# Two key chunks per attention visit for pairs 5, 6 and 7, where there was one

## The chip, the cores and the metric

The kernel runs on one core of one Trainium2 chip. The metric is the device time of one execution in microseconds (us); the time before is the median of three runs. The core's engines are TensorE (PE, matmuls; its weight loads are shown as PEld), VectorE (DVE), ScalarE (ACT), GpSimd (POOL) and SyncE (SP, which issues most DMAs). PE writes its results to PSUM, a small memory in banks, from which DVE or ACT must take them before a bank can be used again.

## What is computed

The program is an attention block with a hash mask, followed by a Fourier mixing block with a feed-forward network. All arrays are float32, the weights come in as float64.

```python
batch, n_heads, seq, head_dim = (4, 8, 768, 64)

# attention: a key counts only if its 6 hash bits equal the query's
q_bits = (np.einsum('bhsd,dk->bhsk', q, proj) > 0)
k_bits = (np.einsum('bhsd,dk->bhsk', k, proj) > 0)
mask = q_bucket[:, :, :, None] == k_bucket[:, :, None, :]
scores = np.where(mask, scale * np.matmul(q, k.transpose(0, 1, 3, 2)), -1e9)
attn = softmax(scores)
x = np.matmul(attn, v)            # then (B,H,S,D) -> (B, S, H*D)

# mixing: real part of a 2-D FFT, normalisation, feed-forward 512 -> 2048 -> 512
mixed = np.real(np.fft.fft(np.fft.fft(x, axis=1), axis=2))
u = x + mixed
un = (u - mean(u)) / np.sqrt(var(u) + 1e-06)
out = u + np.maximum(un @ w_ch1, 0.0) @ w_ch2
```

## The kernel before

**Pairs and chunks.** The heads are taken two at a time. There are 4 batches of 4 pairs, so pairs are numbered n = 0 to 15, and batch b has the pairs 4b to 4b+3. The 768 keys of a pair are cut into 6 chunks of 128. For one chunk, `scores` multiplies the keys by all 768 queries, for two query halves g and two heads h: four matmuls (line 894) into two PSUM tiles named `sc`. There are only two such tiles, so one chunk fills them. `weights` (line 905) takes the exponential of each tile on ACT and writes it to a buffer `pk`. `weigh` applies the hash mask on DVE (line 919, one instruction per head): it keeps a weight where the query's bucket number `qb` equals the key's `kb`. For the first pairs (`LITE`, n = 0 to 4) the mask is added on PE instead, by the bfloat16 matmuls of line 886, and line 919 is not run. `chunk` adds the weights to a running sum `acc` (line 1007). `values` multiplies the weights by the values of that chunk, four matmuls (line 930) into the two tiles `oo`. There are two buffers `pk` (`NPK = 2`), used in turn: a chunk's exponentials can start only when the chunk two before it has been through `values` and the sum.

**The end of a pair.** After the sixth chunk `scale` takes `oo` out of PSUM on ACT (lines 941 and 944), adds up the row sums on PE (line 949), turns them into reciprocals on DVE and, in a second part, spreads them with eight small copies on ACT (line 965) and multiplies the result (line 970).

**Visits.** `attention(b)` is a generator that yields once for each chunk. It has two forms of visit, chosen by `n < TWO`, with `TWO = 8`.

- Pairs 0 to 7 use the single form. One visit does the scores of one chunk, the exponentials directly with them (line 899), the mask and the sum, and then the values of the chunk before.
- Pairs 8 to 15 use the double form, at even chunks only. It does the scores of chunk c, the values of the earlier of two waiting chunks, the exponentials and the mask of c, the values of the later waiting chunk, and then the scores of chunk c+1, marked `glued`, with its exponentials and mask. Odd chunks only yield.

Waiting chunks stand in the list `pending`; the single form leaves one there, the double form two.

**What runs beside it.** Between the visits of batch b the steps of the mixing block of batch b-1 are issued (`other`, the generator `mix`): the Fourier transforms (lines 1122, 1151, 1165), the first feed-forward product (`inner`, line 1426, with copies on ACT and additions on DVE, lines 1448 to 1477) and the second (`outer7`, line 1306, with lines 1318 to 1367). Both products use a Strassen-like scheme with seven products. At each yield of `attention` as many steps are issued as keep pace, some 2.5 of them. The next pair's queries and keys are prepared in steps of their own (`prepare`: transposes on DVE, line 768; hash bits, line 825; bucket numbers, lines 839 and 849, evacuated at lines 535 and 537). They use the same `sc` tiles as the scores. In batch 1, and only there, the second weight matrix is also converted from float64: POOL issues the loads (line 693), DVE and ACT convert (`narrow`, lines 639 to 656, among them line 647 on ACT, which reads the freshly loaded data in `zraw`), DVE makes the sums of quarters (lines 1272 to 1275), and the first weight matrix is cut up for the later batches (`quarters`, lines 1224 to 1230).

**What sets the order.** For batch 0 the order is that of the program text (`manual_schedule`). From batch 1 on a planner lays the order of every engine in advance, with estimated durations: an instruction that is ready by its reckoning is taken by priority, and priority is the order of the program. `behind()` ties a matmul behind the last one noted in `last[0]` (`issue_after`) and moves its priority forward by `AHEAD = 500`. The later matmuls of one chunk's scores, the values, and all scores of a glued chunk are tied in this way. On the chip each engine then works through its list in that order.

Of the kernel before, what the change touches and what calls it, by code (L numbers as in the profile page):

```python
# [485 lines left out]
def _main(  # L486
# [381 lines left out]
        with tc.issue_after(last[0].ins), tc.high_priority(offset=AHEAD):  # L868
            yield

    TWO = 8

    def scores(n, c, glued=False):

        qt, kt, qb, kb = preps[n]
        pss = []
        ks = slice(c * P, (c + 1) * P)
        heads = [slice(h * D, (h + 1) * D) for h in range(2)]
        for g in range(2):
            qs = slice(g * HALF, (g + 1) * HALF)  # L880
            ps = ps_sc.tile([P, 2, 512], F32, tag="sc", name=f"sc{n}_{g}_{c}")
            if kb is None:

                at = (c + (NT // 2 if g else 0)) % NT * P
                for h, rows in enumerate(heads):
                    nc.tensor.matmul(
                        ps[:, h, 0:HALF], qb[rows, 1, at : at + P],
                        qb[rows, 0, g * HALF : (g + 1) * HALF],
                        start=True, stop=False,
                    )  # L890

            for h, rows in enumerate(heads):
                with behind() if (g + h or glued) and n >= NPAIR else nullcontext():
                    last[0] = nc.tensor.matmul(  # L894
                        ps[:, h, 0:HALF], kt[rows, ks], qt[rows, qs],
                        start=kb is not None, stop=True,
                    )
            if n < TWO:
                weights(pks[npk[0] % NPK], g, ps)
            pss.append(ps)  # L900
        return pss

    def weights(pk, g, ps):

        nc.scalar.activation(  # L905
            pk[:, g, :, 0:HALF], ps[:, :, 0:HALF], AF.Exp, scale=SCALE
        )

    def weigh(n, c, pss):
# [3 lines left out]
        npk[0] += 1  # L913
        for g in range(2) if n >= TWO else ():
            weights(pk, g, pss[g])
# [56 lines left out]
    def attention(b):  # L972
# [11 lines left out]
        for t in range(NPAIR):  # L984
# [8 lines left out]
            def chunk(c, pss):  # L993

                nonlocal first
                pk = weigh(n, c, pss)
                new = pk[:, :, :, 0:HALF]
                sums = [acc]
                if c == 0:
                    first = new  # L1000
                elif c == NT - 1 and b == 0:

                    sums.append(new)
                else:

                    for g in (0, 1) if b == 0 else (slice(0, 2),):
                        nc.vector.tensor_tensor(  # L1007
                            acc[:, g], (first if c == 1 else acc)[:, g], new[:, g],
                            op=ALU.add,
                        )  # L1010
                return n, c, pk, oos, sums

            for c in range(NT):
                if n < TWO:
                    new = chunk(c, scores(n, c))
# [573 lines left out]
def kernel(tc, *args):  # L1589

    cn = {n: tc.nc.inline_tensor(a, name="k_" + n) for n, a in _consts().items()}
    with ExitStack() as ctx:
        large = _main(ctx, tc, *args, cn)
    with tc.If(large > 0, preferred_fallthrough_block=True):
        _any_scores(tc, *args, cn)
# [34 lines left out]
```

## Time and profile before

| | us |
|---|---|
| median of 3 runs | 1098.16 (1097.16 to 1098.83) |
| profiled execution | 1095.54 |
| its span, first to last instruction | 1093.6 |
| PE busy in the span | 1034.4 |
| DVE busy | 788.6 |
| ACT busy | 499.2 |
| score matmuls, line 894 (768 passes) | 153.5 |
| value matmuls, line 930 (768 passes) | 149.2 |
| exponentials, line 905 (192) | 146.8, 0.81 each |
| mask multiplies, line 919 (132) | 129.1, 1.01 each |

A line of the page or of an answer names the line of the program, the engine and the operation, then what is written and what is read, with buffer numbers left out. Each float32 matmul is counted as two passes, so a chunk's four score matmuls are "x8". Matmuls overlap in the pipeline, so what one costs is read from start to start. In a list of waits the columns are the total, the number and the longest wait. In a timeline they are the start, the duration, the instruction, and in brackets the idle time before it with what ended it.

### The profile page before, as it was taken

The numbers are of one execution on the slowest core, as the hardware profiler recorded it, in microseconds if no ns is written. First come the engines' busy times: TensorE is split into PE (matmuls) and PEld (weight loads), VectorE is DVE, ScalarE is ACT, GpSimd is POOL, SyncE is SP. The second block draws the span as 40 slices with busy tenths as digits, with TensorE's granted clock in tenths as the row PEclk, the third lists the DMA queues.
The fourth block names the chain that finished last, engine by engine and source line by source line (L and its number), as shares of the span: only waits on it lengthen the run. The fifth ranks groups of instructions, "written<-read, shape, count | busy, mean of one in ns | idle before, by whom it ended". The sixth has DMA issues, their size and how long they took to land.

```text
span 1093.6 us, 14135 instructions
## 1 busy us (share of the span) xinstructions
PE 1034.4 (95%) x4933; PEld 633.6 (58%) x4933; DVE 788.6 (72%) x1336; ACT 499.2 (46%) x1055; POOL 58.3 (5%) x132
## 2 busy tenths in 40 slices
PE   7989897999989999999999999999999999999996
PEld 3333354446744676545664576645675579768675
DVE  5899968868599978694857786876765875644353
ACT  6987556653276324354325424354415522340420
POOL 0000000002000020010000011001000002100000
PEclk9999999999999999999999999999999999999998
DMA  9755352440056162223063224213123205122401
GB/s 233 216 97 126 63 145 67 164 149 11 20 155 207 43 206 40 54 57 84 15 181 85 63 63 159 44 36 91 25 82 113 76 20 173 54 82 84 129 20 42
DMA packets 175711, 103.14 MB, mean 94 GB/s; under 512 B 129552, under 2 KB 162960, under 8 KB 175632
## 3 DMA queue, kind: packets, MB, share of 16 engines
q1 hardware_dynamic: 169840, 88.65, 30.2%
q0 software_dynamic: 4224, 13.11, 3.8%
q8 instruction: 41, 0.67, 0.2%
q10 hardware_dynamic: 1568, 0.39, 0.2%
q14 instruction: 38, 0.31, 0.1%
HBM read 81.14 MB, written 20.97 MB: 93 GB/s over the span
## 4 chain that ended last, share of the span: by engine, by line
PE 57%; DVE 16%; ACT 4%; issue 2%; DMA 2%; DVEq 0%; ACTq 0%
PE o L1306 23%; PE h_p L1426 18%; PE oo L930 5%; PE sc L894 5%; DVE pk L919 5%; DVE acc L1007 3%; PE cs L1122 2%; DMA zraw<-in_moe_w_ch_dram 2%; PE A L1151 1%; PE B L1151 1%; ACT pk L905 1%; ACT rr L965 1%; PE bits L825 1%; DVE x L1165 1%; DVE h L1464 0%
## 5 line engine op out<-in xcount | busy, mean ns | idle before, releaser
L1306 PE MATMUL o<-w,h 128*128 128x256 f32 x1152 | 258.5, 381 | 2.0 <-DVE w L1318 0.8
L1306 PEld LDWEIGHTS o<-w,h 128*128 128x128 f32 x1152 | 216.8, 190 | 41.8 <-issue 3.5
L905 ACT ACTIVATE pk<-sc 128x768 f32<-128x768 f32 x192 | 146.8, 808 | 93.4 <-PE oo L930 30.6
L1426 PE MATMUL h_p<-x,w 128*128 128x384 f32 x448 | 162.4, 492 | 2.2 <-ACT h L1448 1.7
L894 PE MATMUL sc<-qt,kt 64*128 64x384 f32 x768 | 153.5, 502 | 5.9 <-ACT pk L905 5.6
L930 PE MATMUL oo<-pk,vn 128*64 128x385 f32 (+1 forms) x768 | 149.2, 499 | 6.8 <-DVE pk L919 4.4
L919 DVE SCALAR_TENSOR_TENSOR pk<-qb,kb,pk 128x768 f32<-128x768 bf16 x132 | 129.1, 1010 | 34.3 <-ACT pk L905 34.0
L1426 PEld LDWEIGHTS h_p<-x,w 128*128 128x128 f32 x448 | 82.5, 190 | 67.1 <-issue 6.5
L1007 DVE TENSOR_TENSOR acc<-acc,pk 128x1536 f32<-128x1536 f32 (+1 forms) x72 | 105.7, 1482 | 5.7 <-ACT pk L905 5.1
L1426 PE MATMUL h_p<-w 128*128 128x384 f32 x288 | 106.4, 492 | 3.5 <-ACT w L1463 2.3
L930 PEld LDWEIGHTS oo<-pk,vn 128*64 128x64 f32 x768 | 50.7, 136 | 95.0 <-issue 73.3
L894 PEld LDWEIGHTS sc<-qt,kt 64*128 64x128 f32 x768 | 66.4, 186 | 56.8 <-ACT pk L905 19.1
L1426 PEld LDWEIGHTS h_p<-w 128*128 128x128 f32 x288 | 53.0, 190 | 45.5 <-ACT w L1475 5.1
L1318 DVE SCALAR_TENSOR_TENSOR w<-o,rs,w 128x256 f32<-128x256 f32 x56 | 26.7, 477 | 42.4 <-PE o L1306 42.4
L1336 ACT COPY tq<-o 128x256 f32<-128x256 f32 x24 | 8.9, 372 | 101.8 <-PE o L1306 101.8
L1306 PE MATMUL o<-w 128*128 128x256 f32 x176 | 42.0, 381 | 0.3 <-DVE w L1318 0.3
L1459 DVE TENSOR_TENSOR h<-h 128x384 f32<-128x384 f32 x32 | 17.7, 552 | 29.5 <-ACT h L1458 29.5
L1452 DVE TENSOR_TENSOR h<-h 128x384 f32<-128x384 f32 x32 | 17.7, 553 | 26.8 <-ACT h L1451 26.7
L1306 PEld LDWEIGHTS o<-w 128*128 128x128 f32 x176 | 33.0, 190 | 6.8 <-issue 1.1
L1060 POOL DMA_DIRECT2D out_dram<-w x30 | 16.4, 548 | 376.4 <-ACT tq L1336 146.2
L1325 ACT COPY tq<-o 128x256 f32<-128x256 f32 x24 | 8.9, 369 | 58.4 <-PE o L1306 58.3
L1122 PE MATMUL cs<-ch,z 128*128 128x128 f32 (+3 forms) x192 | 31.7, 317 | 3.0 <-DVE bt L829 1.9
(170 smaller groups left out, 1311.4 us busy)
## 6 DMA issues: line engine op xcount, KB each, us to landing
w<-ad SPq DMA_DIRECT2D x168, 128.0 KB, 2.0
w<-bd SPq DMA_DIRECT2D x42, 512.0 KB, 4.5
zraw<-in_moe_w_ch_dram POOLq DMA_DIRECT2D x16, 512.0 KB, 4.0
bd<-w SPq DMA_DIRECT2D x14, 512.0 KB, 4.2
vn<-in_v_dram SPq DMA_DIRECT2D x32, 192.0 KB, 3.4
qn<-in_q_dram SPq DMA_DIRECT2D x120, 48.0 KB, 2.3
kn<-in_k_dram SPq DMA_DIRECT2D x60, 96.0 KB, 3.1
zraw<-in_moe_w_ch_dram SPq DMA_DIRECT2D x8, 512.0 KB, 5.9
```

The lines of the kernel that those rows point to most:

```text
L894: last[0] = nc.tensor.matmul(ps[:, h, 0:HALF], kt[rows, ks], qt[rows, qs], start=kb is not None, stop=True,)
L905: nc.scalar.activation(pk[:, g, :, 0:HALF], ps[:, :, 0:HALF], AF.Exp, scale=SCALE)
L919: nc.vector.scalar_tensor_tensor(w, qb[:, h].rearrange("p (g s) -> p g s", g=2), kb[:, h, c : c + 1], w, op0=ALU.is_equal, op1=ALU.mult,)
L930: oo = nc.tensor.matmul(oos[g][h * D : (h + 1) * D, 0:w], nat["v", n][:, (2 * c + h) * D : (2 * c + h + 1) * D], pk[:, g, h, 0:w], start=( ...
L1007: nc.vector.tensor_tensor(acc[:, g], (first if c == 1 else acc)[:, g], new[:, g], op=ALU.add,)
L1122: nc.tensor.matmul(ps[:, pc + 2 * lo : pc + 2 * hi - 1 : 2], z[:, cp, pc, par, t * P : (t + 1) * P], ch[:, cp, pc, lo:hi], start=(cp == 0) ...
L1151: nc.tensor.matmul(ps[:, cols], F[:, par, k, t, j * P : (j + 1) * P], sq[:, t, k, cols], start=(t == 0), stop=(t == 1),)
L1306: nc.tensor.matmul(ps, a[:, r], right7[i][:, r], start=start and r == 0, stop=r == HF // 2 - 1, skip_group_check=not start,)
L1318: nc.vector.scalar_tensor_tensor(t[:, cols], src, r, t[:, cols], op0=ALU.mult, op1=ALU.add)
L1426: nc.tensor.matmul(ps, left[:, k], right[i][:, k], start=start and k == 0, stop=k == 1, skip_group_check=not start,)
L1452: nc.vector.tensor_tensor(c21, c12, c21, op=ALU.add)
L1459: nc.vector.tensor_tensor(c22, c21, c22, op=ALU.add)
```

## The change

The bound between the two forms of visit moves from pair 8 to pair 5. Pairs 5, 6 and 7, which are all of batch 1 but its first pair, take the double form. Pair 4, whose mask is added on PE, stays with the single form. The tests `n < TWO` in `scores` (exponentials with the scores) and `n >= TWO` in `weigh` (exponentials there) follow the same constant.

```diff
-    TWO = 8
+    TWO = 5
```

At the passage from pair 4 to pair 5 one chunk is waiting, not two; the double form's first `finish()` (`if len(pending) > 1`) is then left out for that visit. At the end of batch 1 two chunks are waiting, and the loop after the pairs takes them both.

## The prediction

> **What bounds the kernel now.** I read the page's busy table first, then the list of what TensorE (PE) waited for in the stretch that changes, then the same list one batch later, where the new visit form already runs, and last the timelines of one visit of each form.
>
> ```profile
> PE 1034.4 (95%) x4933; PEld 633.6 (58%) x4933; DVE 788.6 (72%) x1336; ACT 499.2 (46%) x1055; POOL 58.3 (5%) x132
> ...
> PE 57%; DVE 16%; ACT 4%; issue 2%; DMA 2%; DVEq 0%; ACTq 0%
> ```
>
> PE is busy for 95% of the span and is 57% of the chain that ended last. A change that removes no arithmetic can win only the 59 us in which PE stands, and what PE loses when it goes from one kind of matmul to another. The change touches pairs 5, 6 and 7. By the places of their matmuls in PE's timeline these run from 154 to 380 us. Each pair ends with its row sum (line 949): pair 4's at 175.37, pair 5's at 243.18, pair 6's at 314.87, pair 7's at 379.90.
>
> PE's busy time by stretch, first of batch 1, then of the same stage in batches 2 and 3 (columns: stretch, its length, then busy us of PE, weight load, DVE, ACT, POOL, granted clock, DMA share, GB/s):
>
> ```profile
> 175.00:390.00 215.00, 201.18 (x861) 116.47 (x860) 180.64 (x328) 109.67 (x237) 16.15 (x29) 0.99 0.35 104
> 433.00:650.00 217.00, 210.89 (x963) 127.00 (x964) 159.45 (x248) 93.14 (x201) 8.07 (x18) 1.00 0.31 76
> 691.00:907.00 216.00, 211.04 (x956) 128.77 (x957) 157.07 (x249) 87.49 (x188) 8.07 (x18) 1.00 0.22 62
> ```
>
> PE stands 13.8 us in batch 1's stretch, with one-chunk visits, and 6.1 and 5.0 us in batches 2 and 3, with two-chunk visits. But batch 1 also gives DVE 21 us and ACT 17 us more to do, for it converts the second weight matrix there. So the difference is not the visits' alone. PE's waits say which part is (first three lines batch 1, then batch 2):
>
> ```profile
> PE sc L894 <- ACT pk L905: 3.6, 2, 2.6
> PE kb L849 <- ACT qb L537: 2.1, 1, 2.1
> PE oo L930 <- DVE pk L919: 1.1, 2, 0.9
> ...
> PE A L1151 <- DVE x L1165: 2.1, 2, 1.6
> PE oo L930 <- DVE pk L919: 0.7, 1, 0.7
> ```
>
> In batch 1 the attention's own waits are 3.6 + 1.1 us, with 0.3 at line 839: 5.0 us. In batch 2 they are 0.7. The other 8.7 us of batch 1 are waits of the conversions, of the key and query preparation and of the feed-forward stage.
>
> **The change part by part.** *Nothing is added or removed.* In both forms a chunk is 4 score matmuls (the trace counts 8 passes), 2 exponentials of 0.81 us on ACT, 2 mask multiplies of 1.01 us and one 1.75 us addition on DVE, and 4 value matmuls. So 18 visits of one chunk become 9 of two. The order changes, and with it five things.
>
> (a) *Fewer changes on PE.* One visit of each form (start, duration, instruction, passes):
>
> ```profile
> 230.66 1.56 PE L894 MATMUL sc<-qt,kt 64*128 64x384 f32 x8
> 232.15 1.51 PE L930 MATMUL oo<-pk,vn 128*64 128x385 f32 x8
> 233.59 1.56 PE L1426 MATMUL h_p<-x,w 128*128 128x384 f32 x4
> ...
> 595.76 1.56 PE L894 MATMUL sc<-qt,kt 64*128 64x384 f32 x8
> 597.25 2.81 PE L930 MATMUL oo<-pk,vn 128*64 128x385 f32 x16
> 599.99 1.56 PE L894 MATMUL sc<-qt,kt 64*128 64x384 f32 x8
> 601.48 2.85 PE L1426 MATMUL h_p<-x,w 128*128 128x384 f32 x8
> ```
>
> From start to start, one chunk alone takes 1.49 + 1.44 us, and the wide matmuls around it lose 0.09 us going in (1.38 in place of 1.29) and 0.11 us coming out (1.40 in place of 1.29): 3.13 us. Two chunks together take 1.49 + 2.74 + 1.49 + 0.09 + 0.11 = 5.92 us, where two single ones take 6.26. That is 0.34 us a visit, 3.1 us over nine. The lower end is zero, where another engine sets the pace anyway. Between 165 and 185 us PE stands over 6 us, so pair 5's first two visits save nothing. I take 7 x 0.34 = 2.4 us.
>
> (b) *The exponentials come under a deadline.* In the single form they are issued with the scores; the next scores are some 10 us off, so ACT can be late. In the double form the first chunk's exponentials may start only when the values of two chunks back have left their buffer, and the second chunk's scores follow two chunks of values. In batch 2 that leaves little (ACT, the same visit):
>
> ```profile
> 598.20 1.51 ACT L905 ACTIVATE pk<-sc 128x768 f32<-128x768 f32 x2 [1.84 <-PE oo L930]
> ```
>
> The first exponential ends near 599.0, and the scores that need its bank start at 599.99: 1.0 us of slack. If ACT holds anything longer at that moment, PE stands, since the second scores are tied behind the values; whatever follows on PE (the feed-forward matmuls) stands too. What can be in the way in batch 1 (ACT's waits, 150 to 390 us):
>
> ```profile
> ACT zraw L647 <- DMA zraw<-in_moe_w_ch_dram: 21.3, 13, 4.2
> ```
>
> ACT stands 13 times, 1.6 us on average and 4.2 at most, before a conversion whose weights have not landed. Five of the nine visits fall where conversions run (three of pair 5 up to 225 us, the first two of pair 7 between 310 and 348). An exponential behind a mean wait and its 0.68 us conversion is late by 2.3 us, 1.3 us beyond the slack. The bounds for five visits are 0 and 6.6 us. Batch 2's list has no wait of scores on line 905 at all, so I take a value nearer to zero: one hit, 1.3 us.
>
> The Trainium skill, page "TensorE: Matmul & The Clock Gate", section on the array's architecture, says that ScalarE and VectorE queues are strictly first in, first out. The row above shows ACT standing before one conversion, and by that rule every exponential behind it waits along; taken for all five visits it would put 6.6 us in place of 1.3, and the sum below would be +2.1 us, 1100.3 us.
>
> (c) *The waits of the single form go.* Of the 5.0 us, batch 2 suggests 0.7 remain, a gain of 4.3. Against it: the longest one (2.63 us at 184.43) came from an ACT that did eight small copies (1.65 us) and then waited 1.23 us for weights, which the change leaves. The other end is no gain. I take half of 4.3, 2.1 us. What is late next there is the feed-forward chain through DVE.
>
> (d) *DVE gets its work in lumps.* Odd chunks are issued one step earlier, so after a visit 2 x (2 x 1.01 + 1.75) = 7.5 us can queue on DVE where 3.8 did. DVE is 47.7 of 50 us busy from 300 to 350 us, and the feed-forward additions behind that lump hold ACT, the PSUM banks and then PE. Pair 6's last chunk leaves that stretch (it runs at 301 now, and would join the visit at 290), pair 7's fourth (348) moves into it, so the load is equal. Bounds: a gain of 3.8 us if only the first happens, a loss of 3.8 if only the second. I take zero.
>
> (e) *The queues and the end.* Loads for the next pair stay at the pair's first step on SP; its value buffer is freed by the same visit as now, so SP stands no longer. POOL issues the weight loads after ACT's line 655 and would be late only if ACT is, which is in (b). A pair's scaling ends one chunk later, about 4 us, but the folding that needs it starts at the fifth step. Batch 1 ends with two chunks of values to do, not one, which adds 1.3 us at 380 us and takes it away earlier; 26 us of output products behind it cover the scaling.
>
> Sum: -2.4 + 1.3 - 2.1 + 0 = -3.2 us. The profiled execution took 1095.54 us, its span 1093.6 and 1.9 around it; it lies 2.6 us below the median of the runs, 1098.16. I put the difference on the median: 1095.0 us.
>
> One bit is the clock's. After the 2.05 us stop at 223.44 (a query preparation held up by ACT) the granted clock is 0.91 and then 0.75 in the 5 us slices from 220 and 225, and some matmuls take 847 ns in place of 486. About 2 us are lost there. Pair 5's last chunk will be issued before that preparation, so the stop may move or go; bounds are a gain of 4 us and another such stop for 4, and I take none.
>
> **The rivals.** *Late exponentials, slower.* The place is the second scores of the visits of pairs 5 and 7, the price 1.3 us each. For it: 13 waits on weights and ACT 37.4 of 50 us busy between 300 and 350. Against it: the same form shows no wait of scores on exponentials in batch 2's stretch. Four or five hits, with none of (c), give -2.4 + 5.2 to 6.6, some +4 us: 1102; with one clock drop, 1106. It decides from the second hit if (c) brings nothing.
>
> *DVE sets the length, no change.* From 296 to 350 us and from 165 to 190 us DVE is at 85 to 95%. What PE saves becomes waiting for the feed-forward additions. The sum is -1 to +1 us: 1097 to 1099. That the planner pulls the visits apart, placing wide matmuls between values and second scores (as it does in batch 2 at 464.76 and 468.55 us), so that the change hardly does what it says, gives the same.
>
> *All waits go.* -3.1 - 4.3 - 4 by the clock: 1087. For it: batch 2's 0.7 us. Against it: the conversions remain.
>
> **How the numbers follow.** 0.2% or 2.2 us is about what a measurement of this kernel can tell from no change. The forecast case (1092 to 1096) has 0.34, all waits gone 0.09, no change 0.20, slower by exponentials or by the lumps of (d) 0.37. That gives faster 0.43, same 0.20, slower 0.37. The range leaves out one in ten on either side: 1087.5 to 1106. The likeliest case's own range is 1092 to 1096.
>
> **What would show it.** Right: in 154 to 380 us, 9 groups of scores, 16 passes of values, scores, and PE standing about 12 us between 175 and 390 in place of 13.8, with scores waiting on exponentials below 2 us. (a) is wrong if feed-forward matmuls stand inside the visits. (b) shows as scores waiting for line 905 above 4 us, beside ACT waiting for weights. (d) shows as feed-forward matmuls waiting for ACT's h and w copies longer than now (3.5 us). The prediction fails above all if the new order moves the conversions: it is the planner's for three engines at once, and a small shift can cost another clock drop.

## The result, and the profile after

The changed kernel takes 1105.88 us (median of 8 runs, 1103.76 to 1111.41), the kernel before 1098.70 (median of 8). The ratio is 1.0074, with a 95% interval of 1.0055 to 1.0092: by the ratio the change costs 8.1 us (the two medians lie 7.2 us apart). The prediction was 1095.0 us, in a range from 1087.5 to 1106. The time is inside the range, by 0.1 us, and on the wrong side of no change.

The page of the changed kernel, its busy times and its chain:

```profile
PE 1039.6 (94%) x4933; PEld 636.9 (58%) x4933; DVE 790.1 (71%) x1336; ACT 499.9 (45%) x1055; POOL 62.3 (6%) x132
...
PE 60%; DVE 13%; ACT 5%; DMA 3%; issue 3%; DVEq 0%; ACTq 0%
```

PE is busy for 5 us more, with the same 4933 passes, in a span that is 13.3 us longer (1106.9 to 1093.6). Of those 13.3 us, 3.1 are lost before 120 us, where both programs do the same; that is this execution's own. The rest can be placed by one kind of matmul that both kernels have: the first transform matmuls (line 1122) that wait for the hash bits in batch 1, and those of batch 2. They start at 139.21 and 409.71 us before, 270.5 us apart, and at 142.35 and 423.32 us after, 281.0 us apart. So the stretch that the change touches is 10.5 us longer in this execution. Of these, 6.4 us are PE standing (18.3 us before, 24.8 after) and 4.0 us are PE busy for longer (252.2 and 256.2 us).

What PE waited for from 115 to 400 us, in the changed kernel:

```profile
PE sc L894 <- ACT pk L905: 9.1, 7, 2.5
PE h_p L1426 <- ACT w L1475: 5.0, 2, 3.5
PE h_p L1426 <- ACT h L1451: 3.7, 2, 1.9
PE oo L930 <- DVE pk L919: 3.6, 2, 2.2
```

The same list of the kernel before, from 115 to 390 us:

```profile
PE sc L894 <- ACT pk L905: 5.1, 3, 2.6
PE oo L930 <- DVE pk L919: 3.0, 3, 1.9
...
PE h_p L1426 <- ACT h L1448: 1.7, 2, 1.5
...
PE h_p L1426 <- ACT w L1463: 1.0, 1, 1.0
```

Before, scores wait 5.1 us for exponentials, values 3.0 for the mask, and feed-forward matmuls (`h_p`) 3.5 for ACT's copies of four lines together (with 0.5 and 0.3 us from lines not shown). After, scores wait 9.1 and the feed-forward matmuls 9.7 (with 0.5, 0.3 and 0.2 us from smaller lines). So the attention waits longer, and the stage beside it waits longer too, by even more. ACT's own waits before weight loads (line 647, 150 to 420 us) went from 21.3 us, 13 times, to 26.6 us, 14 times.

One visit of pair 7, PE and then ACT:

```profile
311.37 1.56 PE L894 MATMUL sc<-qt,kt 64*128 64x384 f32 x8
312.87 2.81 PE L930 MATMUL oo<-pk,vn 128*64 128x385 f32 x16
317.17 1.61 PE L894 MATMUL sc<-qt,kt 64*128 64x384 f32 x8 [1.50 <-ACT pk L905]
318.71 1.56 PE L1426 MATMUL h_p<-bt,tq 128*128 128x384 f32 x4
320.11 1.45 PE L1426 MATMUL h_p<-x,w 128*128 128x384 f32 x4
323.39 1.56 PE L1426 MATMUL h_p<-bt,tq 128*128 128x384 f32 x4 [1.83 <-ACT h L1451]
```

```profile
314.26 0.70 ACT L647 ACTIVATE zraw<-zraw 128x512 int32<-128x512 uint32 x1 [2.30 <-DMA zraw<-in_moe_w_ch_dram]
314.85 0.68 ACT L654 ACTIVATE zraw<-zraw 128x512 f32<-128x512 int32 x1
315.57 0.78 ACT L655 ACTIVATE zraw<-zraw,least 128x512 f32<-128x512 f32 x1
316.23 0.20 ACT L655 ACTIVATION_READ_ACCUMULATOR zraw<-zraw,least 128x1 f32 x1
316.32 1.49 ACT L905 ACTIVATE pk<-sc 128x768 f32<-128x768 f32 x2
```

This is the chain in small. ACT stands 2.30 us before a weight load that has not landed, converts, and only then takes the exponentials of scores that were done at 312.9. The second scores, tied behind the values, stand 1.50 us. And 6 us later the feed-forward matmul stands 1.83 us for a copy (line 1451) that ACT has behind the next conversion.

The stands come with a lower clock, here as means over 5 us (columns: stretch, its length, busy us of PE, weight load, DVE, ACT, POOL, granted clock, DMA share, GB/s):

```profile
185.00:190.00 5.00, 4.34 (x16) 1.94 (x12) 3.87 (x6) 3.84 (x10) 0.00 (x0) 0.52 0.01 3
220.00:225.00 5.00, 1.50 (x10) 0.62 (x3) 2.85 (x6) 1.44 (x3) 0.00 (x0) 0.78 0.87 337
225.00:230.00 5.00, 5.00 (x10) 2.74 (x9) 1.82 (x2) 1.29 (x3) 0.00 (x0) 0.54 0.53 211
```

With 0.80 from 190 to 195 us and 0.71 from 265 to 270, five slices between 150 and 400 us are at 0.80 or below after, where there was one (0.75) before. In finer slices the granted clock is either 1.00 or 0.50. After, it is 0.50 from 185.2 to 192.0, from 222.8 to 229.6 and from 267.1 to 270.5 us, 17.1 us in all; before, from 224.1 to 227.5, 3.4 us. Passes that take up to twice as long there account for PE's longer busy time: half of the 13.7 us more, 6.8 us, is an estimate of the most they can add, and the busy time rose by 4.0.

### The profile page after: what moved, and what is told of

Its sections match the earlier page's. It is cut to its first block, busy times and chain, and to the rows that moved or that the text cites. A ratio compares the mean times of both kernels' runs of the same rounds, so it can differ in the third digit from the quotient of the medians.

```text
span 1106.9 us, 14131 instructions
## 1 busy us (share of the span) xinstructions
PE 1039.6 (94%) x4933; PEld 636.9 (58%) x4933; DVE 790.1 (71%) x1336; ACT 499.9 (45%) x1055; POOL 62.3 (6%) x132
## 4 chain that ended last, share of the span: by engine, by line
PE 60%; DVE 13%; ACT 5%; DMA 3%; issue 3%; DVEq 0%; ACTq 0%
PE o L1306 24%; PE h_p L1426 19%; PE oo L930 6%; PE sc L894 5%; DVE pk L919 5%; DMA zraw<-in_moe_w_ch_dram 3%; DVE acc L1007 3%; PE cs L1122 2%; ACT pk L905 1%; ACT rr L965 1%; PE A L1151 1%; PE B L1151 1%; PE bits L825 1%; DVE x L1165 1%; PE un L1177 1%
## 5 line engine op out<-in xcount | busy, mean ns | idle before, releaser
L894 PE MATMUL sc<-qt,kt 64*128 64x384 f32 x768 | 156.7, 512 | 10.0 <-ACT pk L905 9.7
## 6 DMA issues: line engine op xcount, KB each, us to landing
vn<-in_v_dram SPq DMA_DIRECT2D x32, 192.0 KB, 3.5
```

The source lines that it names most:

```text
L894: last[0] = nc.tensor.matmul(ps[:, h, 0:HALF], kt[rows, ks], qt[rows, qs], start=kb is not None, stop=True,)
```

## The experiments

Theory A: weight loads of batch 1 land late, ACT stands before them, and the double form leaves less room for that. Its rivals: B, the clock drops; C, any other order would cost as much; D, the earlier and lumped issue of the work; E, the amount and the order of the work on ACT and DVE, whatever the loads do.

**Which pair costs.** Pair 7 alone, pairs 6 and 7, and pair 5 alone in the double form.

```diff
-    TWO = 8
+    TWO = 7        # and TWO = 6 in the second run
```

```diff
-    TWO = 8
+    DOUBLE = {5} | set(range(8, 16))     # in place of n >= TWO everywhere
...
+                    while len(pending) > 1:
+                        finish()
                     new = chunk(c, scores(n, c))
```

> Only pair 7 of batch 1 in the double form. Between the first of pair 7's scores and the end of batch 1's attention the trace of the changed kernel loses 5.0 us of the 10.5 us that it loses between 154 and 420 us. Theory A (the second scores of a visit are tied behind the values and wait for exponentials on an ACT that stands before late weights): pair 7 lies among conversions, so about half of the whole loss, +3 to +5 us on the time before. Theory B (the stands add up to drops of the granted clock, which are all before 275 us): pair 7 alone costs nothing, -1 to +1 us. Theory C (chance: any other order costs as much): +8 us.

> Pairs 6 and 7 in the double form, pair 5 in the single one. By the landmarks of the two traces pair 6 loses some 3 us and pair 5 some 2.7. Theory A: pair 6's first two visits lie where nothing is converted, so pair 6 adds nothing by waits on exponentials; +3 to +6 us in all. Theory B: pair 6's bunch of visits at 246 to 271 us drops the clock to 0.71, which would cost about 2 us; +1 to +3 us. Theory C: +8 us.

> Pair 5 alone in the double form; where it passes to pair 6's single form one of its two waiting chunks is finished first. Theory A: three visits among conversions, +2 to +4 us. Theory B: the clock falls to 0.52 and 0.80 after the stands at 182 to 187 us of the changed kernel, and to 0.54 after 224, in pair 5's part of the trace; most of the loss, +5 to +8 us. Theory C: +8 us.

| in the double form | ratio to before | 95% interval | us |
|---|---|---|---|
| pair 7 | 1.0052 | 1.0033 to 1.0071 | +5.7 |
| pairs 6 and 7 | 1.0055 | 1.0035 to 1.0075 | +6.0 |
| pair 5 | 1.0021 | 1.0007 to 1.0036 | +2.3 |
| pairs 5, 6, 7 | 1.0074 | 1.0055 to 1.0092 | +8.1 |

The us are the ratio's excess on 1098.7, and each is known to about 2 us. Within that the parts add up: 6.0 and 2.3 make 8.3, and the whole is 8.1. Theory A's expectations hold for pairs 6 and 7 and for pair 5; pair 7 alone costs 0.7 us more than it said. Theory C, which expected +8 of each, falls with pair 5; that any new order costs something is not excluded by these three. Pair 6, whose first two visits run while nothing is converted, adds 0.3 us, which the intervals cannot tell from nothing. Pair 7, whose first two visits run among conversions, costs most; but the number of such visits does not set the price, for pair 5 has three of them and costs 2.3 us. Theory B in its first form, that all is lost by the clock before 275 us, falls too: pair 7 lies after it. A share of the clock remains, and pair 7's own profile shows how it arises. PE, then ACT, in the run of pair 7 alone:

```profile
343.48 1.45 PE L1426 MATMUL h_p<-x,w 128*128 128x384 f32 x4
350.03 2.93 PE L1426 MATMUL h_p<-bt,tq 128*128 128x384 f32 x4 [5.09 <-ACT h L1451]
352.75 4.45 PE L1426 MATMUL h_p<-x,tq 128*128 128x384 f32 x8
```

```profile
344.09 0.69 ACT L647 ACTIVATE zraw<-zraw 128x512 int32<-128x512 uint32 x1 [2.93 <-DMA zraw<-in_moe_w_ch_dram]
345.28 0.68 ACT L654 ACTIVATE zraw<-zraw 128x512 f32<-128x512 int32 x1 [0.49 <-DVE w L643]
345.99 0.76 ACT L655 ACTIVATE zraw<-zraw,least 128x512 f32<-128x512 f32 x1
346.65 0.18 ACT L655 ACTIVATION_READ_ACCUMULATOR zraw<-zraw,least 128x1 f32 x1
346.74 0.65 ACT L647 ACTIVATE zraw<-zraw 128x512 int32<-128x512 uint32 x1
347.29 1.49 ACT L905 ACTIVATE pk<-sc 128x768 f32<-128x768 f32 x2
348.67 0.84 ACT L750 ACTIVATE sq<-kn 128x768 bf16<-128x768 f32 x1
349.41 0.20 ACT L750 ACTIVATION_READ_ACCUMULATOR sq<-kn 128x1 f32 x1
349.50 0.47 ACT L1451 COPY h<-h_p 128x384 f32<-128x384 f32 x1
```

PE had finished the product at 344.9 and needed a PSUM bank back. The copy that frees it (line 1451) is the last of nine records in ACT's list, behind a load that was 2.93 us late, parts of two conversions and the exponentials of the visit's second chunk. PE stood 5.09 us, and the four passes after it took 2.93 us in place of 1.45, at a granted clock of 0.50 (350 to 355 us). In this run no score waits for an exponential from 285 to 410 us; it is the feed-forward stage that waits, 7.1 us on line 1451 alone.

**The lumps without the double form.** Pairs 5 to 7 keep the order of the single form, but two visits are issued at each even step.

```diff
-                    new = chunk(c, scores(n, c))
+                    late = 5 <= n < TWO
+                    for cc in (() if c % 2 else (c, c + 1)) if late else (c,):
+                        new = chunk(cc, scores(n, cc))
                         ...  # the rest of the single visit, once for each cc
```

> Pairs 5, 6 and 7 keep the order of the single form (scores, exponentials with them, values of the chunk before), but two such visits are issued at each even step and none at the odd one. So the work comes in the same lumps and as early as in the double form, without its tie of the second scores behind exponentials that wait for the values. Theory A (the tie costs): -1 to +2 us. Theory D (the lumps on DVE and ACT and the earlier issue cost, the tie does not): +6 to +9 us, as the changed kernel.

Ratio 1.0029 (1.0015 to 1.0044), +3.2 us: between the two expectations. Issuing the same work earlier and in pairs costs something by itself. The rest, some 5 us, is by subtraction the double form's order. Neither A nor D is the whole of it by this run. Its profile does not show the 3.2 us as waits. In the stretch between the two transform matmuls (275.2 us) PE stands 16.0 us, less than the 18.3 before, and is busy for 259.2 us in place of 252.2: the clock is at 0.50 for 10.2 us in place of 3.4, which can account for 3.4 of the 7.0 us at most (an estimate), and where the others come from stays open.

**The loads left out.** The first pair of runs left out fourteen of the sixteen loads.

```diff
-            self.fetch(i + self.depth)
+            if self.col == 0:
+                self.fetch(i + self.depth)
```

> The kernel before with only the first two loads of the second weight matrix; the fourteen later ones are left out and every conversion reads what is already there, so the weights, and the output, are not the reference's. ACT then never stands before a load in batch 1. Theory A (late loads hold ACT, and with it the exponentials and the feed-forward copies queued behind): the form before has some slack, -1 to -5 us against the time before. Theory E (it is the amount and order of work on ACT and DVE, not the loads): 0 to -1 us.

> The changed kernel with the same fourteen loads left out (the output is not the reference's). What counts is its distance to the run beside it, the kernel before without these loads. Theory A: the 8 us of the change shrink to between -3 and +2 us. Theory E: the distance stays at +6 to +9 us.

Both took about 3077 us (ratios 2.80 and 2.79). The stale data looked like unusual weights, the flag of line 655 was raised, and the program computed everything again in its fallback; so the output came out right, other than the expectations say, and the times tell nothing. The main path in the two profiles can still be read by the transform matmuls: 266.7 us from batch 1 to batch 2 in both, against 270.5 in the kernel before and 281.0 in the changed one. The next pair has the flags of these conversions written elsewhere, so that the main path is timed alone:

```diff
-            accum_out=strange[:, col : col + 1]
+            accum_out=(strange if col < 16 else unread)[:, col : col + 1]
```

> As the earlier run of the kernel before without the fourteen later loads of the second matrix, but with the flags that its conversions raise for unusual weights (line 655) written to a tile that nothing reads. In the earlier pair the stale data raised the flag and the program took its fallback for any input after the main path, which tripled the time; the two main paths could only be compared in the profiles, where both took 3.8 us less than the kernel before from batch 1's first transform matmuls to batch 2's, and 0.0 us apart. The output is not the reference's. Theory A (late loads): -2 to -5 us on the time before. Theory E (order and amount of work on ACT and DVE): 0 to -1 us.

> The changed kernel with the same edit (the output is not the reference's). Theory A: within 2 us of the run beside it, where the change costs 8 us with the loads. Theory E: +6 to +9 us beside it.

Single form 0.9970 (0.9958 to 0.9982), double form 0.9962 (0.9947 to 0.9978). Without the loads the change costs nothing (-0.9 us), where with them it costs 8.1 us. A's two expectations hold; E expected +6 to +9. What PE waits for without the loads, 150 to 420 us, first the single and then the double form (line numbers are those of these kernels, one or two above):

```profile
PE oo L932 <- DVE pk L921: 3.2, 3, 2.1
PE sc L896 <- ACT pk L907: 2.0, 3, 1.0
PE h_p L1428 <- ACT u L1180: 1.5, 1, 1.5
```

```profile
PE sc L896 <- ACT pk L907: 6.0, 8, 1.9
PE oo L932 <- DVE pk L921: 3.4, 2, 2.2
PE h_p L1428 <- ACT u L1180: 1.4, 1, 1.4
```

The double form still waits 4.0 us more for its exponentials, eight times, 1.9 us at most; with the loads, in the same window, it waits 3.8 us more (9.1 and 5.3). So the deadline of part (b) is real without any late load, and in sum late loads did not lengthen it. That it eats what the fewer changes on PE save (3.1 us) is not shown: between the transform matmuls PE stands 15.2 us in the single form and 15.3 in the double. What is gone are the long stands of the feed-forward stage: it waits 2.7 us for ACT's copies in the double form, where it waited 9.7 with the loads. One reservation: the planner counts on the loads as well, so without them it lays the conversions at other places in ACT's and DVE's lists (in the double form's two traces some 70 of ACT's 1340 records stand elsewhere in the order). The pair shows that the loss hangs on the loads; it does not separate their landing late from the places that the planner gives the conversions because of them.

**ACT relieved.** First the instruction that waits for the load goes to POOL, then the two instructions of the test for unusual weights are left out as well.

```diff
-        nc.scalar.activation(low, lo.bitcast(U32), AF.Copy, scale=2.0**-29)
+        if col < NDC * DFF // WC:
+            nc.scalar.activation(low, lo.bitcast(U32), AF.Copy, scale=2.0**-29)
+        else:
+            for part in range(low.shape[1]):
+                nc.gpsimd.tensor_scalar(
+                    low[:, part], lo[:, part].bitcast(U32), 2.0**-29, None, op0=ALU.mult
+                )
...
+        if col < NDC * DFF // WC:      # second pair only: lines 654 and 655
```

> The kernel before with the first ACT instruction of each conversion of the second matrix (line 647, the one that waits for the load) on POOL. The waits for loads then stand in POOL's queue, which only issues loads and stores and makes small scalars in batch 1. Theory A: ACT is freed, -1 to -5 us. Theory E: within 2 us of the time before; if the POOL instruction is slow (several us), conversions come late and the time rises.

> The changed kernel with line 647 of the second matrix's conversions on POOL. Theory A: the distance to the run beside it (the kernel before with the same move) falls from +8 us to between -3 and +2 us, and this may be the fastest of all. Theory E: the distance stays at +6 to +9 us.

> The kernel before with no conversion work on ACT in batch 1: line 647 runs on POOL for the second matrix, and its test for unusual weights (lines 654 and 655) is left out. DVE still waits for loads. If late loads and conversions act through ACT's list: -3 to -7 us on the time before. If they act through DVE's list: as the run with line 647 on POOL alone, -3 to -6 us, no better.

> The changed kernel with the same edit. If the loss of the change goes through ACT (exponentials and feed-forward copies queued behind conversions), nothing of it is left and the saving of 0.34 us a visit shows: -3 to +1 us beside the run of the kernel before with the same edit. If it goes through DVE (masks, sums and feed-forward additions queued behind conversions that wait for loads): +3 to +8 us.

| conversions of batch 1 | single form | double form | difference |
|---|---|---|---|
| as they are | 1 | 1.0074 (1.0055 to 1.0092) | 0.74% |
| line 647 on POOL | 0.9952 (0.9937 to 0.9967) | 0.9995 (0.9984 to 1.0006) | 0.43% |
| nothing on ACT | 0.9982 (0.9968 to 0.9996) | 1.0020 (1.0008 to 1.0031) | 0.38% |
| without 14 loads | 0.9970 (0.9958 to 0.9982) | 0.9962 (0.9947 to 0.9978) | -0.08% |

With line 647 on POOL the cost of the change falls from 8.1 to 4.7 us, between what A and E expected. Taking the rest of the conversion off ACT brings it only to 4.2, inside the range that had been set for a loss through DVE (+3 to +8). So by these ratios ACT's list carries about half of the loss, and I was wrong to look for all of it there. The half is rough: by the intervals the drop of 3.4 us is uncertain by some 3 us. And the single form, which gains 5.3 us by moving line 647 (A: 1 to 5), gains only 2.0 with nothing converted on ACT (3 to 7 was expected), which no run explains.

What PE waits for in the profiles from 150 to 420 us, in us, first the single and then the double form:

| conversions of batch 1 | scores on exponentials | feed-forward matmuls on ACT's copies | values on the mask |
|---|---|---|---|
| as they are | 5.3, 9.1 | 3.5, 9.7 | 3.0, 3.6 |
| line 647 on POOL | 1.9, 6.2 | 4.9, 4.2 | 4.7, 5.3 |
| nothing on ACT | 1.9, 2.4 | 5.4, 3.3 | 5.9, 8.4 |
| without 14 loads | 2.0, 6.0 | 3.3, 2.7 | 3.2, 3.4 |

The feed-forward stage waits longer in the double form only where ACT itself waits for the loads. The scores wait some 4 us longer wherever ACT still converts, late loads or not, and 0.5 us longer where it converts nothing. The waits do not give the whole of the times, though. With line 647 on POOL the stretches between the transform matmuls are 269.1 and 270.5 us in the two profiles, only 1.4 us apart, where the ratios of all runs say 4.7 us.

The other half goes another way, and the last run (double form, nothing converted on ACT) shows two stands of it. The longest is that of values on the mask in pair 5:

```profile
171.50 3.75 PE L937 MATMUL oo<-pk,vn 128*64 128x385 f32 x8 [5.68 <-DVE pk L926]
```

The two masks that it needs start at 170.20 us on DVE, which has been busy since 156.4 us, but for one wait of 0.87 us for a load, with conversions, quarter sums, the masks of the chunk before and additions of the transform. The second stand, ACT, then DVE:

```profile
317.55 0.52 ACT L1472 ACTIVATE h<-h 128x384 f32<-128x384 f32 x1 [4.96 <-DVE h L1471]
317.98 0.46 ACT L1474 COPY h<-h_p 128x384 f32<-128x384 f32 x1
```

```profile
311.67 1.01 DVE L926 SCALAR_TENSOR_TENSOR pk<-qb,kb,pk 128x768 f32<-128x768 bf16 x1
...
313.30 1.00 DVE L926 SCALAR_TENSOR_TENSOR pk<-qb,kb,pk 128x768 f32<-128x768 bf16 x1
314.23 0.41 DVE L1281 TENSOR_TENSOR w<-w 128x256 f32<-128x256 f32 x1
314.56 0.68 DVE L643 SCALAR_TENSOR_TENSOR w<-zraw,w 128x512 int32<-128x512 int32 x1
```

DVE is busy without a gap from 306 to 319 us, with the masks of two chunks, conversions and quarter sums. The feed-forward addition (line 1471 there) comes at 316.98, ACT stands 4.96 us for it, and PE stands 3.84 us before a row sum, behind ACT's next copy. That is the lump of part (d). The edits also move the places of conversions on DVE, so how the other half divides between lumps on DVE, loads that DVE and POOL wait for, and the clock stays open.

The kernel before with line 647 on POOL beats both kernels: 1094.68 us (median of 5) beside 1098.74, ratio 0.9952.

## Why the prediction was wrong

- **What bounds the kernel**: right. PE is the bound. But the loss is not standing alone: of 10.5 us, 6.4 are PE standing and 4.0 are PE busy for longer with the same matmuls, at a lower clock.
- **(a) fewer changes on PE, -2.4 us**: the price per visit was right where a visit runs through: 364.97 to 370.69 us is 5.72 us from the first scores to the next stage, as in batch 2. But of the nine visits only two run so. Four have a stand before their second scores (1.40, 0.65, 1.50 and 1.04 us), one before its last values (2.15), and two of pair 5 are pulled apart by the planner.
- **(b) late exponentials, +1.3 us**: the deadline came, and the size is inside its bounds (0 to 6.6), but too small: the four stands make 4.6 us. Its reason is not borne out in sum. It priced an exponential behind a wait for a load, and the visit of pair 7 above has one; but without these waits the scores of the double form wait as much longer than those of the single form (4.0 us, 3.8 with the loads). The difference shrinks to 0.5 us only where ACT converts nothing, so it goes with the conversion work as such. "One hit" was taken because batch 2's list shows none, and batch 2 converts nothing.
- **(c) waits of the single form go, -2.1 us**: this step failed outright. In the prediction's own stretch (175 to 390 us, to 400 after) the attention's waits went from 5.0 to 8.5 us. From 115 us on, scores on exponentials went from 5.1 to 9.1 us, values on the mask from 3.0 to 3.6. Batch 2's 0.7 us did not come with the form; it was measured in a stage without conversions. An ACT without conversions alone does not bring it either: then the scores of the double form wait 2.4 us, but the values 8.4. The sentence that named this risk (the longest wait came from ACT waiting for weights) was worth more than the half I then took.
- **(d) lumps, 0 us**: this is the term that failed by most. Feed-forward matmuls waited 3.5 us on ACT's copies before and 9.7 after, and 2.7 in the double form without fourteen of the loads. I let one chunk that leaves the dense stretch pay for one that enters it; what counted was not the load of DVE over 50 us but how long a queue stands in front of one copy or one addition when PE needs its bank. In the stand of 5.09 us shown above that queue is ACT's, with a late load in it, and not DVE's, as (d) had it; DVE's shows only in the last run. The lumps alone measured +3.2 us, but not as this wait: in that run the feed-forward matmuls wait 4.4 us on ACT's copies.
- **(e)**: nothing in the runs speaks against it. POOL waited longer behind ACT's line 655 before it issued loads (86.7 us in place of 70.2), but for everything before these loads together it waited 176.5 us in place of 185.9. So it is not shown that a late conversion makes the next load late.
- **The clock**: I took none. The profile of the changed kernel has 17.1 us at 0.50 between 150 and 400 us in place of 3.4, and its eight runs order by clock: 1111.4 and 1110.1 us at a mean of 0.984 and 0.985, 1108.9 at 0.989, 1103.8 to 1106.7 at 0.991 to 0.994. A stand can cost twice, as standing and as slower passes after it.
- **The rivals**: the one that came is "late exponentials, slower", at 1102 us, or 1106 with a clock drop, which is the time measured. That the number fits is in part luck: the clock was halved three times, two more than before and not one more, and the greater part of the longer waits is paid at the feed-forward copies and not at the scores. Both signs that the prediction had named came: scores waiting above 4 us, and feed-forward matmuls waiting longer than 3.5.

One place in the Trainium skill bears on this, the strict first-in, first-out order of ScalarE and VectorE on the page "TensorE: Matmul & The Clock Gate", in the section on the array's architecture. Taken for all five visits it had given 1100.3 us, on the right side, but by a wait of the exponentials that the runs do not put on the loads. The nine ACT records above agree with the rule: the copy of line 1451 could have started at 344.9 us, when its product was done, and started at 349.50, after the eight before it.

## What to carry to other kernels

A form that works well in one stage takes its price from that stage: before carrying it over, ask which engine's list is different in the new place, above all whether something in it waits for a load. On an engine that works through its list in order, a wait for a DMA delays everything behind it, so look at who is behind, and count the stand at the copy that frees a PSUM bank and not only at the instructions that were moved. An order with slack (exponentials directly after the scores, next scores 10 us off) was worth more in this stage, with its irregular arrivals, than 0.34 us per visit saved on PE.

## What the runs showed of the hardware

The clock fell after stands shorter than I would have thought. Stands of 2.05 us (up to 223.44, kernel before), 2.15 us (up to 267.09, changed kernel) and 2.46 us (up to 184.61, changed kernel) were each followed, within 0.7 us, by a granted clock of 0.50 that lasted 3.4 or 6.8 us. In a stand of 3.50 us (220.58 to 224.08, changed kernel) the clock fell 2.2 us after its start. But a stand of 2.63 us (up to 184.43, kernel before) was followed by none: the clock is 1.00 from 180 to 190 us. So the length of a stand alone does not decide it here. The same page of the Trainium skill, in its part on what is happening at the clock gate, speaks of an idle window of about 3.4 us before the clock is halved. A stand of 5.09 us gave 0.50 in the next 5 us, so the halving agrees; in these traces shorter stands were enough. Also, one instruction of 0.68 us moved from ACT to POOL, where its two halves take about 1.1 us each, made the kernel 0.48% faster, although POOL then stood over 40 us before loads: the place of this wait counted for more than the price of the work. Taking two more instructions off ACT did not add to it (0.9982).
